# A new written-out order for 1,143 tasks: attention, then a two-layer mixer, on one core

## The chip, the core and the metric

The kernel runs on one core of a Trainium2 chip. The metric is the time of one execution on the device, in microseconds (us). A core has engines that each run their own list of instructions, in order: TensorE (PE; its weight loads are shown as PEld), VectorE (DVE), ScalarE (ACT), GpSimd (POOL) and SyncE (SP). SP issues transfers only; ACT and POOL issue some as well. Transfers that SP starts stand in one queue (q1 in the profile), those of ACT in another (q10) and those of POOL in a third (q0); all three are served by the same 16 DMA engines. Engines wait for each other, and for transfers, by semaphores.

## The reference

For 4 batches, 8 heads, 768 positions and 64 values per head:

```
scores = q @ k.T / 8, kept where the key is one of the first 4 (sinks)
         or one of the last 128 positions up to the query
x   = softmax(scores) @ v              -> (batch, 768, 512), heads side by side
a1  = alpha1 * x + beta1
tok = w_tok (768 x 768) @ a1           mixes the positions
u   = x + lam * tok
a2  = alpha2 * u + beta2
ch  = relu(a2 @ w_ch1 (512 x 2048)) @ w_ch2 (2048 x 512)
out = u + lam * ch                     float32
```

## The kernel before

**Tasks and lists.** The kernel doesn't loop over its work as it issues it. It first makes a list of 1,143 tasks with `add` (each a small function that issues one to some twenty instructions, numbered in the order in which they are made), and then `emit` (L54 to L74) issues them as four tables say:

- `ORDER` (L216) lists the task numbers in the order of issue. An engine runs its instructions in this order.
- `ENGINES` has a digit for each task: 0 ACT, 1 DVE, 2 PE, 3 POOL, 4 SP.
- `HOMES` has the number of the buffer that each tile takes, out of a fixed set for each kind (8 `nat`, 4 `vnat`, 12 `x`, 4 `wst`, 4 PSUM banks `d` and so on).
- `IDLES` puts filler matmuls on a tile of zeros (`warm`, L146 to L148) in front of a task: (task, PSUM bank, how many).

The framework adds only the waits that data and buffers need, and one more: the transfers of SP and ACT take eight completion semaphores by turns, so a transfer isn't issued before the eighth one ahead of it has landed. The arguments `wait=` of the load functions are notes for whoever made the tables; by themselves they put no wait on the chip.

**Stages.** All four batches go through the same stages, with TensorE's lists interleaved:

- Loads: `load_qk` (tiles `nat`, or `n16` where POOL's transfer casts to 16 bits on the way), `load_v` (`vnat`), `load_v0` for batch 0, `load_wtok` (`wtn`, 384 KB each, L435), `load_w1` (L448: the first layer's weights in four quarters of 512 KB as 16-bit values into `w1f`, cast on the way, so issued by POOL; tasks 32 to 35), `load_w` (`wst`, pieces of the second layer's weights, L444).
- `gate(i)` (L452 to L457, tasks 36 to 38) is a tiny SP transfer that reads a piece of quarter i of `w1f`. SP therefore stands at it until that quarter has landed, and everything behind it in SP's list is issued later.
- Transposes of q and k: on TensorE for batches 0 and 1 (`tp`, L504 and L507), by a transposing transfer on SP for batches 2 and 3 (`qkT`, L523).
- Scores `S`, exponentials `E` on ACT, masks, products `pv`, and normalisation into `x` (DVE, L743 and L744). For batch 0 POOL multiplies `x` by alpha1·lam into `xh` (L753), twelve half tiles.
- `tok` (L849): TensorE multiplies `wtokT`, the transposed w_tok (`wT`, L809), with `xh`; DVE adds to `x` (L856); a cast gives `u16`. Then u is transposed into `uT`: on TensorE for batch 0 (`uTp`, L890), by a transposing SP transfer for batches 1 to 3 (`uTx`, L908), each followed by the affine step with alpha2 and beta2.
- `h` (L929): 16 products of four matmuls per half batch; product fi needs quarter fi // 4 of w1. Relu on ACT or DVE.
- The second layer: plain (`ch`, L1114) for batch 0; for batches 1 to 3 seven products `P1` to `P7` (L1046) on sums and differences of halves. Last an addition into `x` (L1059 or L1125) and a store.

**The order around the change.** On POOL the four w1 quarters stand together, behind the first `xh` multiply. On SP, behind the last `wtn` load, come w2 piece 0, the load of lam, w2 piece 12, then gate 1, w2 piece 4 and the loads of batch 1; gate 2 stands among these. On TensorE the first products of the first layer are h 1, 11, 8, 13 of half 0 (quarters 0, 2, 2, 3).

The softmax here doesn't subtract the row's maximum and nothing guards it: scores larger than these inputs give would overflow.

## Time and profile before

| | us |
|---|---|
| runs | 258.48, 256.46, 258.13 |
| median of the runs | 258.13 |
| span of the profiled execution | 254.3 |
| TensorE busy in it | 245.6 |
| DVE busy | 190.7 |
| ACT busy | 133.2 |
| POOL busy | 103.2 |
| first `tok` product starts | 31.39 |
| first `h` product starts | 39.83 |
| last addition on DVE | 250.08 |

The profiled execution's own time isn't given apart from its span; the median of the runs lies 3.8 us above that span. The span runs from the first instruction to the last. The granted TensorE clock was 0.997 of full speed on average. In the lines of the chain of waits the first number is the start, the second the length, both in us; in the timelines the same, followed by engine, line, operation, tiles and count, and in brackets the idle time ahead of it and what ended it. The names are tiles: `w1f<-in_moe_w_ch_dram` is the transfer of w1 into its tile.

### The profile page before, as it was taken

To read this page: it belongs to the slowest core of one execution; us is meant where nothing else is said; L and a number is where in the kernel's file an instruction comes from. 1 tells how busy PE (TensorE), PEld (TensorE's weight loads), DVE (VectorE), ACT (ScalarE), POOL (GpSimd) and SP (SyncE) were. 2 spreads that over 40 slices of the span, in tenths; PEclk is the share of its full clock that TensorE was granted. 3 is DMA by queue.
4 is the path that set the end of the run, shared out by engine and by line. 5 is a ranking of instruction groups with operands and counts; after the bars stand their busy time and mean duration, and the time that the engine had idled before them with its cause. 6 is when DMAs were issued, how large, how long until landed. Compare 5 with 4: busy or idle time off the path is not lost.

```text
span 254.3 us, 5499 instructions
## 1 busy us (share of the span) xinstructions
PE 245.6 (97%) x2167; PEld 159.9 (63%) x2167; DVE 190.7 (75%) x402; ACT 133.2 (52%) x219; POOL 103.2 (41%) x124
## 2 busy tenths in 40 slices
PE   7799997999999999999999999999999999999993
PEld 7554644666555544566687686667667676667882
DVE  5688986767888874978879995578778983228892
ACT  2599913879977034787833434566660235543000
POOL 8318845876455527515782040065662120000010
PEclk9999999999999999999999999999999999999998
DMA  6999999899999999998484764520000140100327
GB/s 182 205 215 266 272 269 316 246 377 300 221 158 233 234 208 156 195 249 180 110 170 107 128 122 138 144 65 0 3 0 3 30 84 13 41 0 3 117 73 268
DMA packets 86129, 38.79 MB, mean 153 GB/s; under 512 B 73540, under 2 KB 80460, under 8 KB 86104
## 3 DMA queue, kind: packets, MB, share of 16 engines
q1 hardware_dynamic: 66576, 28.06, 47.3%
q10 hardware_dynamic: 15784, 7.11, 11.8%
q0 software_dynamic: 3744, 3.28, 8.0%
q8 instruction: 17, 0.28, 0.4%
q14 instruction: 8, 0.07, 0.1%
HBM read 29.91 MB, written 6.29 MB: 142 GB/s over the span
## 4 chain that ended last, share of the span: by engine, by line
PE 84%; DMA 11%; DVE 2%; POOL 1%; SPq 0%; issue 0%
PE h L929 32%; PE P L1046 22%; PE tok L849 9%; PE ch L1114 8%; DMA w1f<-in_moe_w_ch_dram 8%; PE pv L718 3%; PE S L617 3%; DMA nat<-in_k_dram 3%; PE tp L507 1%; POOL w1f L448 1%; PE tp L504 1%; DVE qkT L157 1%; DVE E L696 1%; PE pv L711 1%; PE pv L604 1%; PE idle L148 0%
## 5 line engine op out<-in xcount | busy, mean ns | idle before, releaser
L929 PE MATMUL h<-uT,w1f 128*128 128x384 f16 x512 | 89.8, 326 | 1.5 <-DMA w1f<-in_moe_w_ch_dram 1.5
L929 PEld LDWEIGHTS <-w1f 128*128 128x128 f16 x512 | 48.2, 98 | 32.7 <-DMA w1f<-in_moe_w_ch_dram 1.9
L935 ACT ACTIVATE hT<-h 128x384 f16<-128x384 f32 x77 | 37.0, 491 | 39.5 <-PE h L929 39.3
L937 DVE TENSOR_SCALAR hT<-h 128x384 f16<-128x384 f32 x51 | 27.8, 555 | 23.4 <-PE h L929 22.8
L1046 PEld LDWEIGHTS <-hT 128*128 128x128 f16 x408 | 39.5, 98 | 6.7 <-issue 0.2
L639 ACT ACTIVATE E<-S 128x1024 f16<-128x1024 f32 (+1 forms) x39 | 38.1, 1001 | 7.6 <-PE S L617 6.3
L762 POOL TENSOR_TENSOR tm<-x,la_b 128x512 f32<-128x512 f32 x18 | 24.3, 1353 | 24.2 <-DVE x L744 12.3
L849 PE MATMUL tok<-xh,wtokT 128*128 128x512 f16 x144 | 33.0, 379 | 0.0
L1059 DVE TENSOR_TENSOR x<-x,P 128x256 f32<-128x256 f32 x45 | 18.3, 419 | 11.3 <-PE P L1046 10.2
L1046 PE MATMUL P<-w2f,hT 128*128 128x256 f16 x216 | 26.5, 273 | 0.0
L849 PEld LDWEIGHTS <-wtokT 128*128 128x128 f16 x144 | 13.9, 98 | 15.0
L1114 PE MATMUL ch<-w2f,hT 128*128 128x512 f16 x96 | 23.2, 379 | 0.0
L1046 PE MATMUL P<-w2s,hT 128*128 128x256 f16 x192 | 23.1, 273 | 0.0
L1082 POOL TENSOR_TENSOR x<-x,pt 128x256 f32<-128x256 f32 x4 | 3.4, 854 | 47.5 <-DVE pt L1077 47.5
L155 ACT CAST u<-x 128x512 f16<-128x512 f32 x15 | 9.2, 615 | 24.9 <-DVE x L856 24.3
L744 DVE TENSOR_TENSOR x<-pv,rec 128x256 f32<-128x256 f32 x48 | 20.4, 425 | 1.7
L155 ACT CAST n<-nat 128x768 f16<-128x768 f32 x21 | 16.9, 828 | 8.9 <-DVE x L1125 6.4
L718 PEld LDWEIGHTS <-E 128*128 128x128 f16 x328 | 14.8, 98 | 5.1 <-issue 1.1
L856 DVE TENSOR_TENSOR x<-x,tok 128x512 f32<-128x512 f32 x24 | 16.0, 683 | 2.3 <-PE tok L849 2.3
L718 PE MATMUL pv<-vfs,E 128*128 128x65 f16 x328 | 17.7, 194 | 0.0
L579 POOL TENSOR_SCALAR_AFFINE_SELECT E<-E 128x512 f16<-128x512 f16 x12 | 7.5, 648 | 20.6 <-ACT E L639 20.6
L743 DVE RECIPROCAL rec<-pv 128x4 f32<-128x4 f32 x48 | 8.6, 179 | 7.2 <-PE pv L718 6.9
(134 smaller groups left out, 340.6 us busy)
## 6 DMA issues: line engine op xcount, KB each, us to landing
wst_w<-in_moe_w_ch_dram SPq DMA_DIRECT2D x8, 512.0 KB, 8.2
nat<-in_q_dram SPq DMA_DIRECT2D x10, 384.0 KB, 3.9
vnat<-in_v_dram SPq DMA_DIRECT2D x14, 256.0 KB, 5.7
nat<-in_k_dram SPq DMA_DIRECT2D x8, 384.0 KB, 7.2
out_dram<-x SPq DMA_DIRECT2D x11, 256.0 KB, 3.1
out_dram<-x ACTq DMA_DIRECT2D x10, 256.0 KB, 3.7
wtn<-in_moe_w_tok_dram SPq DMA_DIRECT2D x6, 384.0 KB, 4.1
w1f<-in_moe_w_ch_dram POOLq DMA_DIRECT2D x4, 512.0 KB, 15.4
```

Of the source, the lines that this page charges most:

```text
L155: nc.scalar.copy(o, i)
L639: nc.scalar.activation(eT.t, pS.t[:, :, 0 : n * w].rearrange("p e (i w) -> p e i w", i=n), AF.Exp, scale=scale)
L718: nc.tensor.matmul(po.t[:, hl, :], eT.t[:, e_, off + i, c : c + P], vf[j][:, h, :], start=(r < 2 and n == 0), stop=(n == len(parts) - 1 an ...
L744: nc.vector.tensor_mul(bx.t[:, 4 * G : 4 * G + 4, :], po.t[:, :, 0:D], rec.t.to_broadcast([P, 4, D]))
L762: engine[e].tensor_mul(bt.t, bx.t.rearrange("p h d -> p (h d)"), la1_b)
L849: nc.tensor.matmul(pt.t, wtokT[:, si, ti * P : (ti + 1) * P], hs[si].t, start=(si == 0), stop=(si == NR - 1))
L929: nc.tensor.matmul(ph.t, w1f[:, c, fi * P : (fi + 1) * P], bu.t[:, c, chk * NTOK : (chk + 1) * NTOK], start=(c == 0), stop=(c == NC - 1))
L935: nc.scalar.activation(bh.t[:, fi, :], ph.t, AF.Relu)
L937: nc.vector.tensor_scalar_max(bh.t[:, fi, :], ph.t, 0.0)
L1046: nc.tensor.matmul(pc.t, hh[:, nt * P : (nt + 1) * P], w(fi), start=(first and n_ == 0), stop=(n_ == HF - 1), skip_group_check=True)
L1059: nc.vector.tensor_add(row(bx)[:, cols], row(bx)[:, cols], pc.t)
L1114: nc.tensor.matmul(pc.t, bh.t[:, fi, nt * P : (nt + 1) * P], w2f[:, fi, :], start=(fi == 0), stop=(fi == NF - 1))
```

## The change

`ORDER`, `ENGINES`, `HOMES` and `IDLES` are replaced. Nothing else differs: the same tasks with the same instructions. The tables are some 90 lines of numbers; this is their beginning, and the fillers in full.

```diff
     ORDER = (
-        26, 6, 9, 7, 10, 5, 11, 8, 18, 15, 72, 19, 1, 12, 3, 0, 4, 2, 22, 14, 73, 74, 45, 48, 46,
-        17, 39, 49, 47, 53, 13, 40, 50, 41, 90, 95, 43, 91, 51, 54, 103, 52, 16, 44, 61, 104, 42,
...
+        26, 6, 0, 7, 15, 11, 8, 10, 9, 3, 12, 19, 5, 45, 72, 1, 46, 43, 47, 73, 18, 14, 48,
+        2, 49, 13, 4, 41, 51, 50, 39, 52, 90, 103, 91, 16, 74, 53, 104, 95, 54, 96, 100, 92,
...
     IDLES = (
-        (73, 0, 65), (46, 0, 12), (49, 1, 1), (90, 3, 10), (61, 3, 2), (109, 3, 3), (92, 3, 1),
-        (166, 1, 4), (162, 0, 1),
+        (46, 0, 65), (49, 3, 7), (92, 0, 12),
     )
```

Read as lists of the engines, what differs around the first layer is:

| list | before | after |
|---|---|---|
| POOL | xh, w1 quarters 0, 1, 2, 3, then eleven xh | xh, quarter 0, xh, quarter 1, two xh, quarter 2, eight xh, quarter 3 |
| POOL, earlier | identity made after the masks | identity first; multiplication alpha1·lam (task 39, DVE before) |
| SP behind the last `wtn` load | w2 piece 0, lam, w2 piece 12, **gate 1**, w2 piece 4, one q/k load of batch 1, one v load, q/k loads | q/k load of batch 1, w2 piece 12, five q/k loads of batch 1, one v load (lam is loaded earlier) |
| gates on SP | 1 and 2 in the first fifth of the order, 3 among the transposes of batch 1 | 2 and 3 among the transposes of batch 2 and 3, 1 among those of batch 3 |
| ACT's own loads | q/k loads 8, v 4, w2 0, stores 12 | q/k 8, v 7, w2 3 (pieces 0, 4, 6), stores 7 |
| SP's loads and stores | q/k 18, v 26, w2 8, stores 15 | q/k 18, v 23, w2 5, stores 20 |
| TensorE, first layer | h 1, 11, 8, 13, 12, 14, … | h 11, 4, 1, 8, `uTp`, 14, `uTp`, 13, … |
| TensorE, w_tok transposes | all six before the first `tok` | the sixth behind six of the `tok` tasks |
| filler matmuls | 99 | 84 |

In the second half of the order, plain loads of batch 3 stand between the transposing transfers of batch 1 on SP (one v and one q/k load behind the first three `uT` transposes), and the transposes and products are in other turns throughout; tasks by engine change from DVE 331, ACT 235, POOL 107, SP 111 to DVE 343, ACT 216, POOL 115, SP 110, with 359 on TensorE in both.

## The prediction

> **What bounds the kernel now.** I read the page first, for busy time and for the chain that ended last.
>
> ```profile
> span 254.3 us, 5499 instructions
> PE 245.6 (97%) x2167; PEld 159.9 (63%) x2167; DVE 190.7 (75%) x402; ACT 133.2 (52%) x219; POOL 103.2 (41%) x124
> PE 84%; DMA 11%; DVE 2%; POOL 1%; SPq 0%; issue 0%
> w1f<-in_moe_w_ch_dram POOLq DMA_DIRECT2D x4, 512.0 KB, 15.4
> ```
>
> TensorE is busy for 97% of the span, and the chain is TensorE for 84% of it. Of the 11% of DMA, the line part of the chain gives 8% to the load of `w1f` alone. So I opened the chain over the first 50 us (start, length, what), and then TensorE's timeline around its end.
>
> ```profile
> 20.27 0.74 POOL xh L753
> 21.01 2.22 POOL w1f L448 x3
> 23.23 20.17 DMA w1f<-in_moe_w_ch_dram
> 43.45 2.12 PE h L929 x12
> ...
> 250.08 0.42 DVE x L1059
> ```
>
> ```profile
> 39.83 2.11 PE L929 MATMUL h<-uT,w1f 128*128 128x384 f16 x12
> 43.45 2.12 PE L929 MATMUL h<-uT,w1f 128*128 128x384 f16 x12 [1.50 <-DMA w1f<-in_moe_w_ch_dram]
> ```
>
> Three `h` products run from 39.83, then TensorE waits 1.50 us for the fourth quarter of w1, which lands at 43.40. It is the only long wait that TensorE has after its first `tok` product (31.39): from 43.45 until about 250 it runs from one product to the next. So everything ahead of 43.45 matters only through **the landing of the last w1 quarter**, and everything behind it only through TensorE's own work and new holes in it. I read next what decides that landing, on SP (start, length, what):
>
> ```profile
> 20.87 1.45 SPq L435 DMA_DIRECT2D wtn<-in_moe_w_tok_dram  x3
> 26.07 0.38 SPq L444 DMA_DIRECT2D wst_w<-in_moe_w_ch_dram  x1
> ...
> 27.00 0.43 SPq L444 DMA_DIRECT2D wst_w<-in_moe_w_ch_dram  x1
> 35.96 0.80 SPq L455 DMA_DIRECT2D gates<-w1f  x1
> 36.82 0.40 SPq L444 DMA_DIRECT2D wst_w<-in_moe_w_ch_dram  x1
> 37.34 0.39 SPq L397 DMA_DIRECT2D nat<-in_q_dram  x1
> ```
>
> After 27.43 SP issues nothing until 35.96. What holds it is `gate(1)`, which reads a piece of quarter 1 and so waits for its landing, 35.95. Only then come the loads of batch 1 (`nat`). I counted the trace's transfer records by queue and microsecond (POOL's ring against SP's). While SP has work, from 30 to 37, the two take about equal turns: 105/84, 92/94, 101/101, 94/95, 100/100, 96/93, 101/94, at 367 to 385 GB/s read. Then SP's ring is empty and w1 has the engines to itself: 194, 208, 204 records in the microseconds from 37, 38 and 39, at 399 to 418 GB/s. By 40 all but stragglers of w1 is through; the last quarter lands at 43.40, 3 us after its bulk. Quarters 0 to 2 landed 1.5 us or more after theirs.
>
> **The change, part by part.** The task list is the same. Counted from the two programs, the real columns that TensorE streams are the same, 568,808 (237.0 us at 0.4167 ns each), so what can move is holes, fillers and switches of tile shape.
>
> *The gates and the early loads* (the part that decides). In the new order SP has no gate before its batch-1 loads: the three gates now stand among the `qkT` transposes of batch 3 or later. So after the last `wtn` loads SP issues one quarter of w2 and six `nat`, whose buffers are free by 19 us, as soon as the `v0` cast (about 25) and the completion of earlier loads let it: by about 29 us, where before it stood at gate 1 until 35.96. ACT, which loaded no w2 before, issues two w2 pieces behind its `u16` casts and `wtokT` copies (about 36 and 38) and another with a `nat` about 42: a third ring.
>
> The sum, in bytes read from w1's first record on. Before, it starts at 23.9, 2.9 us after its first issue (20.96); now that issue stands behind a POOL multiply at 22.0 or so, and the first record comes at 24.9. From there w1 has 4.19 MB; SP's ring the rest of `wtn` 0.7 (0.9 were left at 23.9 before), w2 0.5, five to six `nat` 2.0; ACT about 0.9 by then. That is 8.3 MB. At 385 GB/s it takes 21.6 us and ends at 46.5. Counted in records, SP's ring has about 2,100 ahead of its small `vnat` ones, w1 has 2,048: at equal turns neither empties much before the other, so w1 gets no time alone. To this comes the lag from bulk to landing, 1.5 to 3.1 us in before's quarters: quarter 3 lands at 48.0 to 49.6. I take **48.3**, in the lower part, because one `nat` may come behind w1.
>
> TensorE's new order runs h11, h4, h1, h8 and one `uTp` before its first product on quarter 3 (h14), one h (0.65) and one `uTp` (0.34) more than the three h before. It has 0.99 us less left to do when it restarts. The shift of all that follows is (48.3 + 0.05 − 0.99) − 43.45 = **+3.9 us**. Bounds: landing as early as 45.5 gives +1.1 (w1 gets two turns for one of `nat`, whose records are 1,536 bytes against 2,048: between 10 and 16 us the turns of small records against POOL's ran from one to six); 50.5 gives +6.1.
>
> [...]
>
> *First part, fillers and xh chain: nothing.* Idle fillers fall from 99 to 84 (15 at 53 ns, −0.8 us), tile-shape switches before the first `tok` from 52 to 45 (7 at 106 ns, as they take in the trace, −0.74), one weight transpose `wT5` moves behind the first `tok`. The `la1` multiply moves to POOL. The first xh multiply then comes at 21.3 to 22 (20.27 before), but only one w1 start, not four (3.05 us), is ahead of the next ones; the twelve multiplies end about 32.5 (32.87 before). The first `tok` starts at 31.0 or so, the first h at 39.7 to 39.8. The wait for w1 hides all of this. If w1 were early, −0.1 would be left of it, since xh and not TensorE would bound `tok`; if xh were early too, at most −1.5.
>
> *Behind 45 us.* Loads moved from SP to ACT and stores from ACT to SP are issues on engines with slack (52% and 41% busy for ACT and POOL). What can open a hole is the transposing chain from a `tok` product to the first h: add, cast, SP's transpose, affine. For batch 1 it took 6.2 us (96.77 to 102.97); TensorE's cover in the new order is 6.3 (6.6 before). For batch 3 it took 9.9 with cover 10.9; the new cover is 9.1. SP now puts a plain `nat` and a `vnat` between batch 1's first three transposes and the other three; these cover 8.4 against 7 to 8.6 needed (landing 3.7 to 4.9 before). So 0 to 1.5 us more; I take 0, since the same chains in before show slots of SP busy with other transposes that the new order removes. The tail (last add, store, 4 us) is the same.
>
> The profiled execution spans 254.3, the median of the runs is 258.13, 3.8 more, which I carry over: 258.13 + 3.9 = **262.0**.
>
> **Rivals.**
>
> *No hole for w1* (the other side: not slower). If w1 gets more than its equal turn, or the `nat` loads are held on SP by a completion I misjudge until about 36, quarter 3 lands by 42.7, when TensorE reaches h14 (39.75 + 2.95). Then the wait of 1.50 is gone, and what is late next is the xh chain: 258.13 − 1.6 = 256.5; with an earlier xh chain up to 255.1. For it: POOL's ring took the larger share at 28 and 29 (173/28, 192/11), but there SP's ring had run low. Against it: seven microseconds of equal turns. It decides from a landing at 42.7.
>
> *As before.* Quarter 3 lands at 43.4 to 45, because its last packets lag less with a fuller ring or SP's issues are slower: −1.0 to +0.6, so 257.1 to 258.7. That the change doesn't do what it says belongs here: turns by packet are taken already in before, an order can't set them, it can only set what is queued.
>
> *Slower still.* The transposing chains of batches 1 and 3 open holes of 0.5 to 1.5 on top: 262.5 to 265.
>
> **How the numbers follow.** One per cent, about what can be told from no change, is 2.6 us: below 255.5 is faster, above 260.7 slower. The forecast (260.7 to 263.5) has 0.50, slower still 0.13, as before 0.17 (with the low end of the landing, up to 260.7, in it), no hole 0.20, of which 0.07 lies below 255.5. So faster 0.07, same 0.30, slower 0.63. The range runs from 256.0, which leaves out most of the far end of no hole, to 265.5, the late landing with part of the later holes.
>
> **What would show it.** Right: in the new profile, TensorE waits on `w1f` before an h product for 4 to 7 us in all around 40 to 48, SP's `nat` loads are issued before 30, the last w1 landing is behind 47, and from there to the end the time is as before (206 us). Wrong: a w1 landing at or before 43; or new waits of h on `uT` near 105 and 215; or a first `tok` that starts more than 1 us from 31.

## The result, and the profile after

The changed kernel takes 266.55 us (median; 265.01 to 267.67) against 257.72 us (256.46 to 258.48): a ratio of 1.0347, 95% interval 1.0281 to 1.0412. It is slower, as forecast, but by 8.8 us and not by 3.9, and beyond the range. In all ratios and intervals, runs more than 1.5% above the fastest of the same kernel are left out. The profiled spans differ by 11.0 us, 265.3 against 254.3. In every execution taken later the run's time lies 1.7 to 2.4 us above its span, so before's profiled execution, at 254.3, lies near its shortest run (256.46), and after's, at 267.17, near its longest (267.67). The 11.0 us are what the two traces can explain.

Of the page of the kernel after, the busy times, the granted clock and the chain's shares:

```profile
PE 249.3 (94%) x2152; PEld 161.2 (61%) x2152; DVE 200.7 (76%) x418; ACT 122.4 (46%) x195; POOL 109.4 (41%) x134
...
PEclk9869999989999999999999999999999999999998
...
PE 75%; DVE 10%; DMA 9%; POOL 4%; issue 1%; DVEq 0%
```

TensorE's share of the chain fell from 84 to 75%; DVE's rose from 2 to 10%, POOL's from 1 to 4%. The row of the clock has two dents, an 8 and a 6 in the second and third slice (6.6 to 20 us) and an 8 in the ninth (53 to 60). Before had no record at half speed until 252.87, behind its last product. After, the chain of waits (start, length, what) and TensorE's timeline around the end of w1:

```profile
29.88 4.78 POOL xh L757 x7
34.65 16.33 DMA w1f<-in_moe_w_ch_dram
```

```profile
43.94 2.77 PE L933 MATMUL h<-uT,w1f 128*128 128x384 f16 x16 [1.58 <-DMA w1f<-in_moe_w_ch_dram]
...
51.03 0.82 PE L933 MATMUL h<-uT,w1f 128*128 128x384 f16 x4 [3.98 <-DMA w1f<-in_moe_w_ch_dram]
```

TensorE waits twice for w1 instead of once: 1.58 us for quarter 2, which the first product of the new order (h 11) needs, and 3.98 us for quarter 3, which lands at 50.98. SP's queue of the kernel after answers to the list in which gate 1 stood:

```profile
23.52 0.56 SPq L401 DMA_DIRECT2D nat<-in_k_dram  x1
27.50 0.38 SPq L448 DMA_DIRECT2D wst_w<-in_moe_w_ch_dram  x1
27.92 0.47 SPq L401 DMA_DIRECT2D nat<-in_k_dram  x1
28.50 1.52 SPq L401 DMA_DIRECT2D nat<-in_q_dram  x3
30.11 1.91 SPq L401 DMA_DIRECT2D nat<-in_k_dram  x1
```

No gate holds SP: its six q/k loads of batch 1 (`nat`) are out by 32, while w1 is on its way. The windows view of the same kernel shows the clock (stretch, length, busy us of PE, PEld, DVE, ACT and POOL with the number of instructions, granted clock, DMA share, GB/s):

```profile
12.00:14.00 2.00, 1.59 (x17) 0.87 (x16) 1.90 (x3) 1.19 (x2) 0.01 (x1) 0.50 1.31 224
...
48.00:50.00 2.00, 0.00 (x0) 0.00 (x0) 0.00 (x0) 0.27 (x1) 0.00 (x0) 1.00 1.12 337
...
52.00:54.00 2.00, 2.00 (x10) 1.09 (x9) 0.86 (x2) 0.27 (x1) 2.00 (x2) 0.50 0.11 31
...
56.00:58.00 2.00, 2.00 (x14) 1.22 (x13) 1.43 (x4) 1.34 (x4) 0.00 (x0) 1.00 1.06 384
```

Half the clock is granted from 10.85 to 17.68 and, behind the hole, from 51.8 to 55.2: TensorE then runs 10 instructions in 2 us where it runs 14 at the full clock.

**Where the 11.0 us come from.** I measured TensorE's lag: how far it is behind the kernel before when both have streamed the same number of real columns (without those of the fillers). The lag is 2.3 us at the first `tok` (33.42 against 31.39, with one transpose less done), 2.5 when the first h could start, 6.6 at 51, 8.3 from 55.6 on, 8.2 until about 116 and 11.0 from 200 to the end. So there are four terms: **the first 42 us, 2.5; the waits for w1, 5.56 − 1.50 = 4.1; the half clock behind them, 1.7; the stretch from 104 to 215, 2.8** (TensorE is busy there for 109.14 of 111 us, and was for 111.00 before; the other 0.9 us are not idle time). They make 11.1, which is 11.0 but for rounding.

### The profile page after: what moved, and what is told of

Same layout as the page of the kernel before. It is cut to its first block, busy times and chain, and to the rows that moved or that the text cites. A ratio compares the mean times of both kernels' runs of the same rounds, so it can differ in the third digit from the quotient of the medians.

```text
span 265.3 us, 5485 instructions
## 1 busy us (share of the span) xinstructions
PE 249.3 (94%) x2152; PEld 161.2 (61%) x2152; DVE 200.7 (76%) x418; ACT 122.4 (46%) x195; POOL 109.4 (41%) x134
## 4 chain that ended last, share of the span: by engine, by line
PE 75%; DVE 10%; DMA 9%; POOL 4%; issue 1%; DVEq 0%
PE h L933 28%; PE P L1050 18%; PE ch L1118 8%; PE tok L853 8%; DMA w1f<-in_moe_w_ch_dram 6%; PE S L621 3%; POOL xh L757 3%; PE pv L722 3%; DMA lb_b<-in_moe_beta_dram 3%; DVE E L658 1%; PE tp L511 1%; DVE lb_b L1168 1%; PE tp L508 1%; POOL w1f L452 1%; DVE hT L994 1%
## 5 line engine op out<-in xcount | busy, mean ns | idle before, releaser
L933 PE MATMUL h<-uT,w1f 128*128 128x384 f16 x512 | 91.8, 330 | 6.4 <-DMA w1f<-in_moe_w_ch_dram 5.6
L933 PEld LDWEIGHTS <-w1f 128*128 128x128 f16 x512 | 48.6, 99 | 38.6 <-DMA w1f<-in_moe_w_ch_dram 6.2
L939 ACT ACTIVATE hT<-h 128x384 f16<-128x384 f32 x75 | 35.9, 495 | 42.6 <-PE h L933 42.4
L1050 PEld LDWEIGHTS <-hT 128*128 128x128 f16 x408 | 39.6, 98 | 7.6 <-issue 0.7
L157 POOL CAST u<-x 128x512 f16<-128x512 f32 x12 | 8.6, 720 | 38.8 <-DVE x L860 36.5
L155 ACT CAST u<-x 128x512 f16<-128x512 f32 x12 | 7.4, 616 | 35.9 <-DVE x L860 35.9
L722 PE MATMUL pv<-vfs,E 128*128 128x65 f16 x328 | 16.9, 193 | 0.0
L1118 PEld LDWEIGHTS <-hT 128*128 128x128 f16 x96 | 8.7, 98 | 9.4 <-issue 0.4
L157 POOL CAST vfs<-vnat 128x512 f16<-128x512 f32 x18 | 12.0, 679 | 4.6 <-DMA vnat<-in_v_dram 4.6
## 6 DMA issues: line engine op xcount, KB each, us to landing
nat<-in_q_dram SPq DMA_DIRECT2D x9, 384.0 KB, 11.7
```

What stands on the lines that cost most here:

```text
L157: engine[e].tensor_copy(o, i)
L722: nc.tensor.matmul(po.t[:, hl, :], eT.t[:, e_, off + i, c : c + P], vf[j][:, h, :], start=(r < 2 and n == 0), stop=(n == len(parts) - 1 an ...
L933: nc.tensor.matmul(ph.t, w1f[:, c, fi * P : (fi + 1) * P], bu.t[:, c, chk * NTOK : (chk + 1) * NTOK], start=(c == 0), stop=(c == NC - 1))
L939: nc.scalar.activation(bh.t[:, fi, :], ph.t, AF.Relu)
L1050: nc.tensor.matmul(pc.t, hh[:, nt * P : (nt + 1) * P], w(fi), start=(first and n_ == 0), stop=(n_ == HF - 1), skip_group_check=True)
L1118: nc.tensor.matmul(pc.t, bh.t[:, fi, nt * P : (nt + 1) * P], w2f[:, fi, :], start=(fi == 0), stop=(fi == NF - 1))
```

## The experiments

The order of the groups is that of the terms, w1 first. "Lag" is the one just defined, and "ring" is used as in the prediction, for the queue of transfers of one issuing engine. Where a run is told with an interval, that is the ratio to the kernel before.

### Who sets the landing of w1

**e1_gate3_first**: after, with SP held in front of its loads of batch 1 until quarter 3 has landed.

```diff
-        215, 212, 218, 88, 216, 226, 230, 179, 219, 177, 89, 161, 197, 220, 171, 185, 223,
+        215, 212, 218, 88, 216, 226, 230, 179, 219, 38, 177, 89, 161, 197, 220, 171, 185, 223,
...
-        722, 592, 581, 588, 593, 888, 913, 916, 583, 594, 742, 743, 731, 595, 919, 732, 38,
+        722, 592, 581, 588, 593, 888, 913, 916, 583, 594, 742, 743, 731, 595, 919, 732, 
```

> The new order with the gate on w1's fourth quarter put in front of SP's first load of batch 1, so that no load of batch 1 and no w2 load of SP is queued until all of w1 has landed. Theory A (the early loads share the rings with w1 and so make TensorE's two waits of 1.6 and 4.0 us): the fourth quarter lands at 41 to 43.5 in place of 50.98, both waits shrink to under 0.5 us together, the half-speed clock behind them goes too, and the span falls from 265.3 to 257 to 259.5; a late batch-1 load may cost up to 1.5 of this again near 55. Theory B (the late issue of the fourth quarter on POOL and the stragglers of w1's own transfer decide, the company doesn't): it lands behind 47 all the same and the span stays within 1.2 of 265.3.

Median 260.64 us, ratio 1.0102 (1.0034 to 1.0170), span 257.4. The quarters land at 31.27, 33.78, 36.32 and 39.24, 11.7 us earlier, and TensorE's timeline of this kernel has no wait for w1:

```profile
41.12 2.76 PE L933 MATMUL h<-uT,w1f 128*128 128x384 f16 x16
...
45.99 0.50 PE L894 MATMUL uTp<-iden,u 128*128 128x128 f16 x6 [1.12 <-ACT hT L939]
```

The clock stays full until TensorE's last product. One task moved in SP's list takes 5.9 us off the median of the changed kernel: theory A. The wait of 1.12 us for ACT is new; g2 takes it up. The head is part of this gain: in this execution the first `tok` lags 1.2 and not 2.3, and quarter 3 is issued at 33.56 and not at 34.65.

**e2_before_ungated**: the other way round, before with its gates 1 and 2 put behind the batch-1 loads, beside gate 3.

```diff
-        210, 153, 217, 179, 211, 178, 157, 197, 229, 36, 212, 215, 218, 185, 216, 226, 230, 219,
+        210, 153, 217, 179, 211, 178, 157, 197, 229, 212, 215, 218, 185, 216, 226, 230, 219,
...
-        278, 267, 37, 260, 271, 358, 268, 198, 285, 349, 272, 381, 301, 286, 366, 351, 303, 302,
+        278, 267, 260, 271, 358, 268, 198, 285, 349, 272, 381, 301, 286, 366, 351, 303, 302,
...
-        632, 463, 653, 356, 651, 656, 627, 332, 38, 654, 480, 333, 342, 624, 652, 473, 310, 476,
+        632, 463, 653, 356, 651, 656, 627, 332, 36, 37, 38, 654, 480, 333, 342, 624, 652, 473, 310, 476,
```

> The order of before with its first two gates moved behind the third one, among the transposes of batch 1; nothing else. Theory A: SP's batch-1 loads are queued by about 30, w1's fourth quarter lands at 45.5 to 48 (43.40 with the gates), TensorE's wait for it grows from 1.5 to 3.5 to 6 us, if it comes over about 3 us a stretch of half clock adds up to 1.7, and the span is 256.5 to 260.5. Theory B: the landing stays at 43 to 44 and the span at 254.3 give or take 1.2, since w1 is issued as early as before.

Median 261.85 us, ratio 1.0163 (1.0088 to 1.0239), span 258.2. Its timeline of TensorE:

```profile
40.86 1.48 PE L929 MATMUL h<-uT,w1f 128*128 128x384 f16 x8 [0.49 <-DMA w1f<-in_moe_w_ch_dram]
45.65 2.84 PE L929 MATMUL h<-uT,w1f 128*128 128x384 f16 x12 [3.31 <-DMA w1f<-in_moe_w_ch_dram]
```

Quarter 3 lands at 45.61 instead of 43.40, the clock is at half from 46.91 to 50.32, and from there the lag stays at 3.87 us: 0.49 + 3.31 − 1.50 of waits and 1.7 of clock make 4.0. Theory A: the missing gate alone turns the kernel before into one that is 4 us slower, with a half clock that no change of TensorE's work caused.

**f1_no_third_ring**: after, with the three w2 loads (tasks 179, 185 and 186) taken from ACT and put at the end of SP's group.

```diff
-        215, 212, 218, 88, 216, 226, 230, 179, 219, 177, 89, 161, 197, 220, 171, 185, 223,
-        231, 221, 172, 232, 222, 224, 176, 225, 170, 169, 279, 227, 257, 280, 233, 173, 228,
-        237, 175, 234, 273, 238, 186, 182, 241, 258, 293, 243, 274, 246, 203, 242, 291, 247,
+        215, 212, 218, 88, 216, 226, 230, 219, 177, 89, 161, 197, 220, 171, 223,
+        231, 221, 172, 232, 222, 224, 176, 225, 170, 169, 279, 227, 257, 280, 233, 173, 179, 185, 186, 228,
+        237, 175, 234, 273, 238, 182, 241, 258, 293, 243, 274, 246, 203, 242, 291, 247,
...
-        "4440413330013114411114433114440402213221021321021121021321320212120120211212020202020202"
+        "4444413334413114411114433114440402213221021321021121021321320212120120211212020202020202"
```

> The new order with the three w2 loads that ACT issues (pieces 0, 4, 6) issued by SP instead, behind its six q/k loads of batch 1, so that only two q/k loads are left to ACT's ring before w1 has landed. Theory A (the third ring takes turns from the last records of w1 after 42): the fourth quarter lands at 46.5 to 49.0 in place of 50.98, TensorE's second wait falls from 4.0 us to 0 to 2, and the span falls by 2 to 4 us. Theory B (two rings are enough for the delay, the last records are held by something of their own): it lands within 0.8 of 50.98 relative to its issue, and the span within 1.2 of 265.3.

One run, 262.71 us, span 260.9 (before beside it: 257.35). Quarter 3 is issued at 34.59, as in after (34.65), and lands at 48.16, 2.8 us earlier. In the seven executions that leave this stretch as it is in after (after, e3, e4, f3, f4, g1, h3) it lands at 49.24 to 51.11, so f1 lies 1.1 us outside their range. The waits for w1 fall to 0.89 and 1.92, and the clock stays full behind them:

```profile
43.18 2.77 PE L933 MATMUL h<-uT,w1f 128*128 128x384 f16 x16 [0.89 <-DMA w1f<-in_moe_w_ch_dram]
...
48.20 0.82 PE L933 MATMUL h<-uT,w1f 128*128 128x384 f16 x4 [1.92 <-DMA w1f<-in_moe_w_ch_dram]
```

Theory A: the third ring adds little bandwidth (355 to 392 GB/s are read with two rings at work from 34 to 42, 383 to 396 with three from 42 to 47) and takes turns from w1: in after the three rings were served 70/67/71 records (POOL, SP, ACT) in the microsecond from 43. A wait of 0.66 us for DVE at 55.22 takes back some of it.

**f2_quarter3_early**: after, with the start of quarter 3 (task 35) directly behind that of quarter 2, before the xh multiplies.

```diff
-        146, 70, 133, 71, 34, 137, 67, 142, 134, 126, 124, 147, 158, 127, 143, 154, 159,
+        146, 70, 133, 71, 34, 35, 137, 67, 142, 134, 126, 124, 147, 158, 127, 143, 154, 159,
...
-        83, 168, 209, 77, 86, 164, 213, 157, 35, 210, 165, 214, 149, 217, 153, 229, 211,
+        83, 168, 209, 77, 86, 164, 213, 157, 210, 165, 214, 149, 217, 153, 229, 211,
```

> The new order with POOL's issue of the fourth quarter of w1 moved from behind the twelve xh multiplications to directly behind the third quarter's issue. Theory A (POOL's ring is never empty before the fourth quarter's records are due, so the issue time doesn't matter): it is issued 5 us earlier, lands within 1 us of 50.98, and the span stays within 1.2 of 265.3. Theory B (the late issue makes the late landing): it lands 3 to 5 us earlier and the span falls by 3 or more.

One run, 264.40 us, span 262.6. Quarter 3 is issued at 26.20, 8.45 us earlier, and lands at 49.65, 1.3 us earlier, which is inside the 49.24 to 51.11 of the executions that leave this alone; the waits are 2.83 and 1.75. Nearer to theory A than to B: an issue 8.45 us earlier hardly moves the landing. The span falls by 2.7 us all the same, but not through the issue of this quarter. The head of this execution happens to run undisturbed (lag 0.3 at the first `tok`), yet the waits for w1 swallow that. What reaches the end is the landing (lag 5.3 at 51, 6.6 in after) and the clock, which is at half from 43.17 to 46.58, ahead of the second wait and hidden by it: from 51 to 56 the lag stays at 5.3, where it grew by 1.7 in after.

**e3_hole_filled**: after, with 72 filler matmuls in the hole.

```diff
-        (46, 0, 65), (49, 3, 7), (92, 0, 12),
+        (46, 0, 65), (49, 3, 7), (92, 0, 12), (293, 2, 72),
```

> The new order with 72 more filler matmuls in front of h product 14, inside the wait of 4 us. Theory A (the idle wait itself lowers the granted clock to one half for 3.4 us afterwards): the clock stays at full speed between 51 and 56, and the span is 1.4 to 1.8 shorter than 265.3, with the wait for w1 as long as before. Theory B (the lower clock has another cause, such as the burst of work behind the wait): the stretch at half speed stays and the span is 265 to 266.

Median 265.11 us, ratio 1.0269 (1.0195 to 1.0344), span 263.2. Behind the hole the clock is full (compare the x14 in 2 us with the row 52 to 54 of the kernel after):

```profile
48.00:50.00 2.00, 2.00 (x40) 2.00 (x38) 0.00 (x0) 0.00 (x0) 0.70 (x1) 1.00 1.09 377
52.00:54.00 2.00, 2.00 (x14) 1.18 (x12) 1.56 (x4) 0.49 (x1) 2.00 (x3) 1.00 0.52 123
```

The lag goes from 6.15 to 6.14 across the same products over which it grows from 6.61 to 8.27 after: theory A, 1.7 us of the loss are the clock.

**g3_before_gate2**: before, with gates 1 and 2 exchanged, so that SP stands longer.

```diff
-        210, 153, 217, 179, 211, 178, 157, 197, 229, 36, 212, 215, 218, 185, 216, 226, 230, 219,
+        210, 153, 217, 179, 211, 178, 157, 197, 229, 37, 212, 215, 218, 185, 216, 226, 230, 219,
...
-        278, 267, 37, 260, 271, 358, 268, 198, 285, 349, 272, 381, 301, 286, 366, 351, 303, 302,
+        278, 267, 36, 260, 271, 358, 268, 198, 285, 349, 272, 381, 301, 286, 366, 351, 303, 302,
```

> The order of before with its first two gates exchanged: SP is held until w1's third quarter has landed, not its second. Theory A (company in the rings sets the landing of the fourth quarter): it lands at 41 to 42.6 in place of 43.40, TensorE's wait of 1.50 us goes to 0 to 0.7, and the span falls by 0.8 to 1.5, unless the batch-1 loads, 2 to 4 us later, open a wait near 54. Theory B (the last records of w1 are late for their own sake, 3 us behind the bulk even with little company): it lands at 42.8 to 43.5 and the span doesn't move by more than 0.7.

Median 255.70 us, ratio 0.9984 (0.9938 to 1.0031), span 255.2: no difference. Quarter 3 lands at 44.30, 0.9 us later than before and outside both theories' bounds, and TensorE waits 1.64 us. SP's ring is empty from 39 to 42 and the last hundred or so records of w1 still trail by 3.7 us: as theory B says, the tail of w1 is there without SP's traffic. But less sharing is not what this run tested: ACT's ring, with a q/k load issued at 37.59, was served 96 and 119 records in the microseconds from 40 and 41. Where no other ring, or hardly one, had work in the tail, the time from 95% of w1's records to the landing was 1.2 us (e1) and 2.2 (h2 below); here and in before, where rings fill up in it, 3.7 and 3.5; in f1, with SP's ring full, 4.0; in after, with both, 6.1. It doesn't grow in proportion: in j1 (below) it was 2.3 with SP's ring at work.

### The first 33 us

**e4_lb_late**: after, with the lb multiply (beta1 by lam, task 41; la is alpha1 by lam) behind the first evacuation of `tp`.

```diff
-        2, 49, 13, 4, 41, 51, 50, 39, 52, 90, 103, 91, 16, 74, 53, 104, 95, 54, 96, 100, 92,
-        109, 42, 93, 28, 94, 97, 110, 61, 24, 44, 101, 62, 55, 63, 98, 107, 17, 102, 56, 30,
+        2, 49, 13, 4, 51, 50, 39, 52, 90, 103, 91, 16, 74, 53, 104, 95, 54, 96, 100, 92,
+        109, 41, 42, 93, 28, 94, 97, 110, 61, 24, 44, 101, 62, 55, 63, 98, 107, 17, 102, 56, 30,
```

> The new order with DVE's multiplication of beta1 by lam moved from in front of the first qkT evacuation to directly before the shuffle that needs it. Theory A (this multiplication waits for its row until 10.25 and takes 2.30 us beside POOL's own multiplication, and so holds the first evacuation, the scores and the first xh back): the first qkT evacuation on DVE starts at 10.0 to 11.0 (12.49 now), the first xh at 22 to 23 (23.92 now), and the span falls by 1 to 2 us, because w1's issues come as much earlier. Theory B (the head is set by the loads and the half clock from 10.9 to 17.7): first xh and span stay within 0.5 and 1.0 of what they are.

Median 265.19 us, ratio 1.0252 (1.0165 to 1.0338), span 263.5. What was wrong is seen in the timelines of the kernel after, DVE first, then POOL:

```profile
10.27 2.30 DVE L1168 TENSOR_TENSOR lb_b<-lb_b,lam_r 128x512 f32<-128x512 f32 x1 [0.20 <-DMA lb_b<-in_moe_beta_dram]
12.49 0.94 DVE L157 COPY qkT<-tp 128x768 f16<-128x768 f16 x1
```

```profile
10.73 1.28 POOL L1168 TENSOR_TENSOR la_b<-la_b,lam_r 128x512 f32<-128x512 f32 x1
```

DVE's multiply takes 2.30 us while POOL does the la multiply, which the change gave to it; before, the same multiply took 0.67. TensorE waits for the evacuation behind it, the copy of the transposed q and k (`tp`) out of PSUM. In e4 DVE's timeline reads:

```profile
11.29 0.96 DVE L157 COPY qkT<-tp 128x768 f16<-128x768 f16 x1 [1.50 <-PE tp L508]
...
14.97 0.69 DVE L1168 TENSOR_TENSOR lb_b<-lb_b,lam_r 128x512 f32<-128x512 f32 x1
```

The multiply is back at 0.69, the evacuation 1.2 us earlier and the lag at the first `tok` 0.8 instead of 2.3: theory A. What reaches the end is 1.6 us (a lag of 9.4 at 215 instead of 11.0), because the landing, 49.24, still decides. The other executions bear it out. In the six whose list has the two multiplies side by side and in which they met (after, e3, f1, f3, f4, g1) the lb multiply took 1.83 to 2.30 us and the lag at the first `tok` was 1.6 to 3.3; in the eight where they didn't meet, by an edit (e4, g2, h1, h3, i1, j1) or by chance (e1, f2), it took 0.68 to 0.69 us and the lag was 0.3 to 1.4. What makes up that rest is not shown.

**g1_head_filled**: after, with 32 fillers instead of 7 in front of task 49.

```diff
-        (46, 0, 65), (49, 3, 7), (92, 0, 12),
+        (46, 0, 65), (49, 3, 32), (92, 0, 12),
```

> The new order with 32 filler matmuls in place of 7 in front of the second transpose of q and k, so that TensorE's idle stretch near 8 to 10 us (1.87) falls to about 0.5. Theory A (the idle stretches of the head bring the half clock between 11 and 18, and this is most of the 2.3 us by which the first tok product is late against before): no stretch at half speed ahead of 20 us, the first tok product late by 0.3 to 1.2 us against 31.39, and the span 1 to 2 us shorter than 265.3 for the head alone. Theory B (the head is late for the loads and DVE's order; the clock only follows): the first tok product stays 2 us late or more though the clock is at full speed.

Median 266.19 us, ratio 1.0397 (1.0335 to 1.0460), span 264.1. Its DVE timeline still has the multiply at 2.15 us, from 10.54. The lag at the first `tok` is 2.1: the fillers that the change dropped are not what is late in the head. How much the half clock adds there this run doesn't settle, since the stretch at half speed was only shortened, from 6.83 to 3.41 us, and theory B had supposed it gone.

**h3_pool_dve**: after, with the la multiply (task 39) back on DVE and two masks of E (706, 958) moved from DVE to POOL.

```diff
-        "3313134433443333444444444444444433334443111211201202121212021213300121211211211200200200"
+        "3313134433443333444444444444444433334441111211201202121212021213300121211211211200200200"
...
-        "2012121312121312134213421040100213421042104111020202120202021202121202020212121212020202"
+        "2032121312121312134213421040100213421042104111020202120202021202121202020212121212020202"
...
-        "4404444044433333304040404043404341202010121203032121332030321213320303212131201012121312"
+        "4404444044433333304040404043404341202010121203032121332030321213320303212131203012121312"
```

> The new order with three steps given back to the engines that had them before: the multiplication alpha1 by lam to DVE, and two score masks (the last of batch 2, the first half of block 4 of batch 3) to POOL. Theory A (a DVE operation beside a two-input operation of POOL takes two to three times as long, and these places pass it on to TensorE): the multiplication of beta1 on DVE takes 0.68 in place of 2.30 us, the first tok product starts 0.8 to 2.0 us earlier than 33.42, and the waits of 0.31 and 0.54 us that were at 139.9 and 195.95 go to under 0.15 each. Theory B (the loads and the clock set the head, and DVE's late places come from its own list): the first tok product stays within 0.5 of 33.42 and the two waits stay.

One run, 264.08 us, span 262.2 (before beside it: 256.85). The DVE timeline of its head:

```profile
9.42 0.68 DVE L1168 TENSOR_TENSOR lb_b<-lb_b,lam_r 128x512 f32<-128x512 f32 x1
10.03 0.68 DVE L1168 TENSOR_TENSOR la_b<-la_b,lam_r 128x512 f32<-128x512 f32 x1
```

Both multiplies on DVE take less (1.36) than one beside POOL's (2.30). The lag at the first `tok` falls to 1.4, and the waits at 139.9 (0.31) and 195.95 (0.54) are gone; the lag that TensorE gathers over the same products as from 104 to 215 in after falls from 2.8 to 1.9 us. Theory A. But the waits for w1 rise to 3.01 and 3.52, since the landing stays at 51.08: a better head alone is given back there.

### Behind 100 us

The third wait of TensorE's table after, `PE h L933 <- DVE uT L879: 0.8, 1, 0.8`, stands on the transposing chain of batch 1. The timelines of the kernel after, DVE and then POOL:

```profile
118.14 0.65 DVE L879 TENSOR_SCALAR uT<-uT,ab 128x384 f16<-128x384 f16 x1
118.72 1.08 DVE L658 TENSOR_TENSOR E<-E,maskn 128x1024 f16<-128x1024 f16 x1
119.73 1.49 DVE L879 TENSOR_SCALAR uT<-uT,ab 128x384 f16<-128x384 f16 x2
```

```profile
117.50 1.76 POOL L157 CAST vfs<-vnat 128x512 f16<-128x512 f32 x3 [4.57 <-DMA vnat<-in_v_dram]
119.23 1.58 POOL L965 TENSOR_TENSOR w2f<-w2f 128x512 f16<-128x512 f16 x1
```

SP's sixth transposing transfer of that batch was issued at 112.96 and had landed at 117.42; it is the affine steps (L879) that are late, 3.1 us for four instructions with the mask. Over the whole trace the mask multiply of 128x1024 takes 0.68 us alone and 1.21 on average beside a POOL multiply, addition or subtraction (seven times), the affine step 0.39 and 0.68 (seven times).

**f3_transposes_first**: after, with two v loads (624, 625) and a q/k load (880) moved behind SP's transposes of this stretch.

```diff
-        472, 481, 628, 463, 353, 482, 658, 473, 331, 624, 348, 880, 653, 659, 332, 654, 471,
-        343, 468, 476, 470, 469, 650, 474, 350, 498, 656, 483, 333, 502, 477, 625, 355, 475,
-        660, 499, 346, 651, 503, 478, 661, 490, 655, 479, 504, 652, 344, 663, 662, 492, 884,
+        472, 481, 628, 463, 353, 482, 658, 473, 331, 348, 653, 659, 332, 654, 471,
+        343, 468, 476, 470, 469, 650, 474, 350, 498, 656, 483, 333, 502, 477, 355, 475,
+        660, 499, 346, 651, 503, 478, 661, 490, 655, 479, 624, 880, 625, 504, 652, 344, 663, 662, 492, 884,
```

> The new order with three plain loads (a v and a q/k load of batches 2 and 3 on SP, a v load on ACT) moved from between the transposing transfers of batch 1 to behind the sixth of them. Theory A (the transposing transfers wait in the ring behind the plain loads, which makes TensorE's wait of 0.84 us for the affine step near 121): the sixth transposing transfer is issued and lands 1 to 3 us earlier, measured from the end of the tok products, the wait goes to under 0.2 us, and the time lost between 100 and 125 falls by 0.6 to 1.0. Theory B (the affine steps are late on DVE, not their input): the wait stays at 0.6 to 1.0 though the transfers land earlier.

One run, 268.83 us, span 267.0. The wait is gone, with the last affine steps and the mask between them in 1.86 us, but POOL's casts of v also moved away from them, because v now lands later; that opens waits of 0.52 and 0.67 us at 125.8 and 131.1, and this execution had a bad head (lag 3.3) and 6.8 us of half clock behind the hole. It doesn't separate SP's transposes from POOL's neighbours.

**f4_sub_on_dve**: after, with one subtraction for the second layer's weights (task 342, L965) moved from POOL to DVE.

```diff
-        "1212120202021212021212021202021212121202122221422221422221022221422221022221433111131111"
+        "1212120202021212021212021202021212121202122221422221422221022221422221022221431111131111"
```

> The new order with one subtraction on w2 (1.58 us on POOL from 119.23) given to DVE, behind the affine steps of batch 1. Theory A (a 16-bit operation of DVE takes up to three times as long while POOL runs a two-input operation, and this makes the wait near 121): the mask beside it takes 0.68 in place of 1.08 us, the last affine steps 0.40 in place of 0.73, and TensorE's wait near 121 falls from 0.84 to 0 to 0.3. Theory B (the affine steps wait for the transposing transfers): these times don't change and the wait stays at 0.6 to 1.0.

One run, 264.82 us, span 263.0. The last two affine steps take 0.95 us together (1.49 after) and the wait falls from 0.84 to 0.60; the mask in front of them, beside POOL's casts, still takes 1.09, and a wait of 0.31 us comes up at 126.9. In part theory A: POOL's work beside DVE is a cause here, moved rather than removed. Over the whole stretch this execution gathers a lag of 3.0 us, no less than after's 2.8.

A gain shows only with h3's two masks. Over the same products the lag grows by 2.4 to 3.5 us in the seven executions without any of these moves (after, e1, e3, e4, f1, f2, g1), by 1.9 with h3's moves alone, and by 1.0, 1.3 and 1.0 in the three below that have both (h1, i1, j1).

### All parts together

**g2_all_parts**: after, with e1's gate, e4's lb multiply, f4's subtraction and g1's fillers. The edits are those shown.

> The new order with four repairs at once: the gate on w1's fourth quarter in front of the batch-1 loads, the multiplication of beta1 late on DVE, 32 fillers in the head, and the one subtraction on DVE. If the parts found so far add up (head 2.3 to under 1, waits for w1 5.6 to under 0.5, half clock behind them 1.7 to 0, the holes behind 100 us from 3.0 to 2.7, and a wait of about 1 us for ScalarE near 46 that the earlier gate run showed), the span is 255.5 to 257.5: still 1 to 3 us above before, from the holes behind 100 us. If something else than these parts is lost, it stays at 258 or more.

Median 260.19 us, ratio 1.0160 (1.0093 to 1.0228), span 258.4: no better than e1. The clock is full everywhere, w1 lands at 40.84, the lag at the first `tok` is 0.8. The largest loss is one new wait; TensorE's timeline and ACT's:

```profile
47.54 0.49 PE L894 MATMUL uTp<-iden,u 128*128 128x128 f16 x6 [3.10 <-ACT hT L939]
```

```profile
41.99 0.61 ACT L155 CAST u<-x 128x512 f16<-128x512 f32 x1
44.95 0.42 ACTq L401 DMA_DIRECT2D nat<-in_k_dram  x1
46.58 0.38 ACTq L448 DMA_DIRECT2D wst_w<-in_moe_w_ch_dram  x1
47.00 0.87 ACT L939 ACTIVATE hT<-h 128x384 f16<-128x384 f32 x2 [4.40 <-DMA wst_w<-in_moe_w_ch_dram]
```

ACT stands from 42.6 to 47.0 at two loads of its own, which may only be issued when the eighth transfer ahead has landed; those are SP's held loads (the one of 42.34 landed at 46.56, and ACT's second load followed at 46.58), and the relu behind ACT's loads waits with them. So a gate on SP, together with loads on ACT, holds TensorE.

**h1_repaired**: g2 with e4's part left out, h3's three tasks moved, and ACT's q/k loads 174 and 175 and w2 load 186 put on SP.

```diff
-        231, 221, 172, 232, 222, 224, 176, 225, 170, 169, 279, 227, 257, 280, 233, 173, 228,
-        237, 175, 234, 273, 238, 186, 182, 241, 258, 293, 243, 274, 246, 203, 242, 291, 247,
-        248, 295, 292, 174, 285, 188, 296, 301, 294, 289, 181, 302, 267, 187, 290, 286, 249,
+        231, 221, 172, 232, 222, 224, 176, 225, 170, 169, 279, 227, 257, 280, 233, 173, 175, 186, 174, 228,
+        237, 234, 273, 238, 182, 241, 258, 293, 243, 274, 246, 203, 242, 291, 247,
+        248, 295, 292, 285, 188, 296, 301, 294, 289, 181, 302, 267, 187, 290, 286, 249,
```

> The new order with six repairs: the gate on w1's fourth quarter in front of the batch-1 loads; the three loads that ACT issued there after 42 (two q/k loads, w2 piece 6) given to SP, so that ACT's relu steps don't stand behind a load that waits; the multiplication alpha1 by lam back on DVE; 32 fillers in the head; one subtraction on w2 given to DVE; and two score masks given back to POOL. If ACT's held loads made the 3.1 us wait near 47 of the four-part repair, that wait goes to under 0.5; the other parts leave a head late by 0 to 1.0, no wait for w1, and 1.5 to 2.5 of the 3.0 us behind 100: span 253.5 to 256.5, the same as before. If the early loads were needed early, a wait for the transposes of batch 1 near 52 to 58 shows instead, and the span is 257 or more.

Median 261.18 us, ratio 1.0150 (1.0086 to 1.0213), span 259.9. No wait for w1 (41.26), none for ACT's loads, the lag at 47 is −0.3. Then the late loads of batch 1 are late themselves:

```profile
55.16 0.51 PE L511 MATMUL tp<-iden,n 128*128 128x128 f16 x6 [3.40 <-ACT n L155]
```

With the half clock behind it (56.1 to 59.5) the lag is 5.6. Over the stretch behind 100 it grows by 1.0 instead of 2.8.

**i1_gate1_repaired**: after with gate 1 in place of gate 3 (task 36 before 171), f2's early quarter 3, h3's and f4's moves and g1's fillers.

```diff
-        215, 212, 218, 88, 216, 226, 230, 179, 219, 177, 89, 161, 197, 220, 171, 185, 223,
+        215, 212, 218, 88, 216, 226, 230, 179, 219, 177, 89, 161, 197, 220, 36, 171, 185, 223,
...
-        984, 985, 998, 840, 834, 991, 855, 36, 999, 992, 989, 1006, 846, 1000, 856, 833,
+        984, 985, 998, 840, 834, 991, 855, 999, 992, 989, 1006, 846, 1000, 856, 833,
```

> The new order with the gate where before had it (on w1's second quarter, in front of all but two of SP's early loads), the fourth quarter issued directly behind the third, the multiplication alpha1 by lam on DVE, the two score masks on POOL and the one subtraction on DVE as in before or the runs above, and 32 fillers in the head. With a gate that lets go of the batch-1 loads near 36, the wait moved to their transposes or to ACT by the later gate should not come: fourth quarter lands at 42.5 to 45, TensorE's waits for w1 together 0 to 1.0, no half clock behind them, no wait over 0.5 between 46 and 60, head late by 0.3 to 1.4, and 1.0 to 1.5 lost behind 100: span 253.5 to 256.0 and the time within 1% of before. If the sum of the parts is not complete, the span is 257 or more.

Median 259.87 us (12 runs), ratio 1.0091 (1.0046 to 1.0135), span 257.3: the lowest ratio among the repairs, though not told apart from e1's 1.0102, and still 0.9% behind before. The quarters land at 30.62, 35.69, 38.75 and 42.19, nothing waits for them, no clock is lost; what is left are 0.48, 0.99 and 1.22 us of waits for ACT, which again stands at its own loads (issued at 43.42, 45.15 and 50.81), and the 1.3 us behind 100.

**j1_act_free**: i1 with ACT's three loads 174, 175 and 186 on SP, by h1's diff.

> The last combined version (gate as in before) with one more change: the two q/k loads of batch 1 and w2 piece 6 that ACT issued between 43 and 51 are issued by SP, behind its other q/k loads. If ACT's loads, each standing until an earlier transfer has landed, hold ScalarE's relu steps and so made TensorE's waits of 0.99 and 1.22 us at 46.1 and 51.8, both go to under 0.3 and the span falls from 257.3 to 255 to 256, unless the transposes of batch 1 now wait for these loads. If the relu steps are late for another reason, the two waits stay at 0.8 or more.

Median 261.14 us, ratio 1.0138 (1.0057 to 1.0220), span 259.2. The waits at 46 and 52 are gone, but the two loads that ACT still has are now issued at 41.87 and 43.98 (37 to 40 in i1), in front of a copy of `wtokT`, and a `tok` product waits for it:

```profile
43.17 2.37 PE L853 MATMUL tok<-xh,wtokT 128*128 128x512 f16 x6 [3.96 <-ACT wtokT L155]
```

The half clock follows, from 43.60 to 47.01. The mechanism is confirmed; the wait is moved, not removed.

**h2_before_gate3**: before, with gate 3 in the place of gate 1, gate 1 in that of gate 3, and two q/k loads of batch 1 (171, 177) put on SP (their digits in `ENGINES` aren't shown).

```diff
-        210, 153, 217, 179, 211, 178, 157, 197, 229, 36, 212, 215, 218, 185, 216, 226, 230, 219,
+        210, 153, 217, 179, 211, 178, 157, 197, 229, 38, 212, 215, 218, 185, 216, 226, 230, 219,
...
-        632, 463, 653, 356, 651, 656, 627, 332, 38, 654, 480, 333, 342, 624, 652, 473, 310, 476,
+        632, 463, 653, 356, 651, 656, 627, 332, 36, 654, 480, 333, 342, 624, 652, 473, 310, 476,
```

> The order of before with the gate on w1's fourth quarter in place of the gate on its second, the first gate sent to where the third stood, and the two q/k loads of batch 1 that ACT issued given to SP, so that no ring but POOL's has anything while w1's last quarters run. Theory A (company in the rings sets the landing): the fourth quarter lands at 39.5 to 42, TensorE's wait of 1.50 us goes to 0 to 0.4, the span falls by 1.0 to 1.5, unless q/k loads that come 3 to 4 us later open a wait near 54. Theory B (the last records of w1 trail 3 us for their own sake, as with the gates exchanged): it lands at 43 to 44.5 and nothing is won.

Median of all 12 runs 262.50 us; the ratio, 1.0104 (1.0048 to 1.0160), is that of five of them. Span 258.5. Quarter 3 lands at 42.43, 1.0 us earlier than before and between the two theories' bounds, and TensorE doesn't wait for it, but comes 5.8 us late itself: its first `h` starts at 45.66. A `pv` product waits 2.00 us for DVE at 31.2, behind a cast of w_tok whose load was issued at 23.0 instead of 21.4, and the clock is at half from 31.45 to 38.28. Why that load, ahead of every edit, is issued later stays open, and so does what the gate is worth without it. No version here beats the kernel before.

## Why the prediction was wrong

**What bounds it: right.** The landing of the last quarter of w1 is the link between the order of the DMA issues and the end, as e1 (11.7 us earlier, no wait) and e2 (before with the same disease) show. The formula for the shift holds too: with the measured landing, (50.98 + 0.05 − 0.99) − 43.45 = 6.6, and the lag at 51 is 6.6. Of the four signs that were to show it right, three are in the trace: waits of 5.56 us in all, a landing behind 47, and SP's `nat` loads issued early, five of six by 30 and the sixth from 30.11. The fourth isn't: from the end of the last wait to the last addition it takes 210.0 us (51.03 to 261.06), not 206. And two of the signs against it came: the first `tok` starts 2.4 us behind 31, and a product `h` waits 0.84 us for `uT`, though at 121 and not near 105.

**The sum for the landing: three terms off, two up and one down.** It said 24.9 (first record) + 21.6 (bulk) + 1.8 (lag) = 48.3. Measured: 27.22 + 17.6 to 95% of w1's 2,048 records, at 44.85, + 6.1 = 50.98.

- The start was 2.3 later, because the head is late (below). Counted the same way, before's first record starts at 23.52, not at the 23.9 of the prediction.
- The bulk was 4.0 shorter. The rate was as assumed, 382 GB/s read, but 6.7 MB passed and not 8.3. Of the rest of `wtn`, put at 0.7 MB, 0.06 was left at the first record; 1.8 of the 2.0 MB of `nat` and 0.36 of ACT's 0.9 had passed by then. "So w1 gets no time alone" was wrong: in the microseconds from 28, 29 and 30 POOL's and SP's rings were served 155/46, 195/12 and 199/0 records. The equal turns were right, and there they were turns by record: from 34 to 42 it was 115/114, 103/97, 111/112, 106/107, 109/119, 108/113, 109/108, 112/113 in each microsecond, though w1's records are 2,048 bytes as read and those of `nat` 1,536.
- The step "the lag from bulk to landing, 1.5 to 3.1 us" failed, and it is the one that makes the landing late: 6.1. With SP's and ACT's rings at work at the end, the last hundred records of POOL's ring trickle at 37, 26, 15, 16, 7 and 5 per microsecond from 45 on. Why they trickle is not shown; that they mostly do so for longer with other rings at work is what e1, h2, f1 and after show side by side (1.2, 2.2, 4.0 and 6.1 us). The third ring was in the sum with 0.9 MB, 2.3 us of bulk at 385 GB/s; taken away in f1 it is worth 2.8 us of landing, of which 2.1 are in this lag.

**"The wait for w1 hides all of this": failed.** It was said of fillers, switches, the la multiply and the xh chain. The first `tok` started at 33.42 instead of 31.0. The la multiply on POOL was costed as a move; it made DVE's lb multiply 2.30 us long instead of 0.67, and that stood in front of the evacuation that TensorE needed (e4, h3; not the fillers, g1). What the half clock in the head adds to this is not priced apart. And w1 could not hide it, because w1's starts stand in the same POOL list behind the first xh: 23.92 instead of 21.3 to 22. What hides a delay must not be delayed by it.

**The clock: not in the sum.** A hole of 4 us was priced at its length. It costs 1.7 us more in the 3.4 us behind it (e3, e2).

**"Behind 45 us … I take 0": failed**, with the bound of 1.5 as well; it was 2.8. The rival "slower still" put holes on the transposing chains; the one at 121 is there, but not because SP's transposes come late: the sixth had landed at 117.42 and DVE's steps ended at 121.2, slow beside POOL (f4, h3, in part). With h3's and f4's moves together 1.0 to 1.3 of the 2.8 is left; that rest I did not take apart.

Added up: 3.9 forecast + 2.7 (landing) + 1.7 (clock) + 2.8 (behind 100) is 11.1, for 11.0 between the spans. The direction came out as forecast, and the rivals "no hole" and "as before" did not happen.

## What to carry to other kernels

Before an early load is moved past a gate, ask whose turns it takes: here two rings with records of 1,536 and 2,048 bytes were served about as many of each (111/112 in one microsecond, 106/107 in the next), so each such ring with work took a share from the transfer that was waited for, and its last records trickled in for longer where the others were full (6.1 us against 1.2). A hole on TensorE must be priced with the half clock that can stand behind it (1.7 us more behind after's 3.98 us; from 25 us on it came with as little as 2.00 us of idle time in a window, as told below), and a delay counts as hidden only if the thing that hides it doesn't depend on it. Moving a multiply from DVE to an idle POOL can cost DVE more than it saves: here it saved 0.7 us and cost up to 1.6.

## What the runs showed of the hardware that I had not expected

**In these traces the clock followed TensorE's idle time in fixed windows, not the length of a hole.** The stretches at half speed within the kernel are 3.41 us long, or 6.83, and where one execution has two, they start a whole number of times 3.413 us apart: 10.85 and 51.81 in after (12.0 times), 13.35 and 44.07 in f4 (9.0 times), 11.82 and 49.37 in e4 (11.0 times). So each execution can be cut into windows of 3.413 us whose edges its own slow stretches give, and TensorE's idle time be summed in each, with fillers counted as work. From 25 us until TensorE's last product, the clock fell at the end of every window with 2.00 us or more of it: 2.00 (h2), 2.08 (g1), 2.15 (e2), 2.39 (f4), 2.46 (h1), 2.62 (after), 2.82 (f2), 2.98 (j1), 3.24 (f3), 3.33 (e4). It fell behind no window with less; the most were 1.92 (f1) and 1.91 (h3). That is why the hole of 2.83 us in f2, which lies in one window, brought the clock down, and those of 3.01 and 3.52 us in h3, each cut in two by an edge, did not. In the head less was enough, 1.62 (f3), while 1.25 (h2) was not. The clock came back after one window where TensorE idled 0.24 us or less in it, and after two where it idled 0.31 or more.

**DVE beside POOL.** An f32 multiply of 128x512 took 1.83 to 2.30 us instead of 0.68 beside one on POOL. In all six executions where the two met, POOL's took 1.28, as it does alone, and DVE's ended 0.56 to 0.57 us behind it, whether DVE had started 0.5 us ahead (after) or at the same time (f1, f4). Summed over DVE's instructions, what they take beyond the shortest of the same line and form is 12.2 us before and 19.4 after. Normalisation and relu, which read PSUM, were not stretched: in after they take 0.42 and 0.55 us both beside POOL's two-input operations (21 and 10 times) and away from them.

**The head has more than one outcome.** With the same program up to that point, the lb multiply does or doesn't meet POOL's (0.69 us in e1 and f2, 1.83 to 2.30 in after, f1, f3 and f4), and the clock is at half for 0, 3.4 or 6.8 us: the lag of the first `tok` is 2.3 in after and 0.3 in f2, whose order is the same up to the start of w1's last quarter. One execution's span can't tell edits of 2 us in these kernels; that is why the landings, waits and lags of each trace carry the readings above.

**Issuing a load is work that can wait.** ACT, busy for 46% of the time in after, held TensorE for 3.1 us in g2 because its next load stood in line for a transfer of SP: that one landed at 46.56, the load was issued at 46.58.
